# A fused attention and mixture-of-experts kernel: the last token group's gating and the first expert products take other places, and two weight splits another engine

## The chip, the cores and the metric

The kernel runs on one core of a Trainium2 chip. The metric is the device time of one execution in microseconds (us). The core's engines run side by side, each in its own instruction order, and wait for each other through semaphores: PE (TensorE: matmuls and transposes), DVE (VectorE), ACT (ScalarE), POOL (GpSimd, which also issues the indirect, row-by-row transfers) and SP, which issues most plain transfers.

## The reference

Linear attention with decay over 4 batches, 8 heads, 768 positions and a head size of 64 gives 3072 tokens of width 512. A noisy top-2 gate then picks two of 8 experts for each token, and each expert is a two-layer network 512 - 1024 - 512:

```
logits = x @ w_gate
noisy_logits = logits + log1p(exp(x @ w_noise)) * noise
top2 = argpartition(-noisy_logits, 2)[:, :2]      # two experts a token
top2_w = softmax over the two
for e in experts:
    h = maximum(x[mask] @ w1[e], 0)
    out[mask] += top2_w[mask] * (h @ w2[e])
```

## The kernel before

**Attention** runs in 12 steps (`NST`, t = 0 to 11), each of two chunks of 128 tokens. Step t's outputs `xo` are taken from PSUM by ACT (L388). Then come `products` (PE L416: the gate's two weight matrices times `xo`; ACT copies the result to `xp`), `turn_x` (8 PE transposes L428 to token rows `xc`), `store_x` (the rows go to `x_tok` in DRAM) and `logits` (PE L447: transposes into the PSUM tile `pL`).

**Routing** works on three groups of 8 chunks. `gate` is a chain of some 50 small DVE instructions (L457, the copy from `pL`, to L498, which writes `ob`). `count` (PE L532 to L537) needs `ob` and numbers the tokens of each expert. `route` (DVE L548 to L612) makes positions; in its middle `finish` issues 24 small PE products (L583), which give the row indices of expert 0's tokens. Then 16 indirect scatters per group (POOL L622) write a record of each token and choice to the list `lst`, 48 in all. `routing` is a generator: `advance(n)` emits its next n DVE instructions at that place of the program, so the FILL numbers say how gate instructions lie between other work.

**Expert 0** starts right after attention, in three passes of 2, 2 and 3 row tiles of 128 tokens. Tile rows are gathered by POOL (L813, `gather_rows`) into `xg`, turned by PE (`trans_rows`, L822) and split into a high part `xth` (ACT) and a low part `xtl` (DVE L825). All expert products are made of three: high x high, low x high, high x low. A pass has 8 columns f (`mm1`, PE L860, 12 matmuls each) into four PSUM buffers `pS`; `evac1` takes each out, the high part of `ht` by ACT (L866), the low part by DVE (L870). `gemm2` (L898, 24 matmuls a tile) follows. Weights come as fp32 in `wst`; ACT writes their high parts (L771, `split_high`) and DVE or POOL the low parts (L775, `split_low`).

**Order and pacing.** Each engine runs the program's order. Before the change the order after the last step is: `products(11)`, `trans_rows` of tiles 0 and 1, `logits(11)`, column 0 (`head[0]`), `turn_x(11)`, column 1, the second group's index products, columns 2 to 7 with the last group's gate between their evacuations on DVE, `gemm2` of tile 0, `count`, `trans_rows` of tiles 2 and 3, `gemm2` of tile 1. The second pass follows: column 0, the last group's index products L583, column 1, and so on. The scatters are spread over the columns: `paced` has POOL copy one element of a fresh `ht` column into `spacer` (L670) before it scatters. After the last scatter, SP loads the record list of the next expert (`rec`), and POOL gathers that expert's rows by it.

Of the kernel before, what the change touches and what calls it, by code (L numbers as in the profile page):

```python
# [31 lines left out]
C = 128  # L32
# [9 lines left out]
TS = 128  # L42
TAILS = (64, 64, 32, 32, 32, 0, 0, 0)
TAIL = max(TAILS)
PARTS0 = (2, 2, 3)
# [9 lines left out]
NST = NCH // 2  # L55
# [1 line left out]
MAXOV = 40  # L57
MAXT = 24
FILLA, FILLB, FILLC = {4: 24, 5: 24, 6: 20, 7: 20, 8: 19, 9: 19, NST - 1: 24}, 2, 4
FILL1, FILL2 = 4, 9  # L60
LOADS = {2: [(1, 0)], 3: [(1, 1)], 4: [(1, 2)], 5: [(1, 3)], 9: [(2, 0), (2, 1)], 10: [(2, 2)], 11: [(2, 3)]}
HIGH = {4: [(1, 0)], 5: [(1, 1)], 6: [(1, 2)], 7: [(1, 3)], 10: [(2, 0), (2, 1)]}
LOW = {5: [(1, 0)], 6: [(1, 1)], 7: [(1, 2)], 10: [(2, 0)]}
# [4 lines left out]
GB = (0, 8, 16, NCH)  # L68
NG = len(GB) - 1
# [14 lines left out]
def size(e, t):  # L84
    return TS if t < NT - 1 else TAILS[e]


def sub(ap, offset, dims):
    return bass.AP(tensor=ap.tensor, offset=ap.offset + offset, ap=dims)
# [27 lines left out]
def kernel(  # L117
# [3 lines left out]
    nc = tc.nc  # L121
# [163 lines left out]
    def finish(b, all_scattered=True):  # L285
        while "done" not in RT.get(b, {}):
            advance(1)
        if all_scattered:
            scatter(len(scatters))

    def scatter(n):
        for job in scatters[:n]:
            scatter_list(*job)
        del scatters[:n]
# [117 lines left out]
    def products(u):  # L412

        p = psum.tile([128, 2, C], FT, name="pR")
        for d in range(DB):
            nc.tensor.matmul(p[d * 32:(d + 1) * 32], wgn[:, d, :], XO[u][:, :, d, :], start=True, stop=True)  # L416
        XP[u] = aw.tile([128, 2, C], FT, name="xp", bufs=1)
        nc.scalar.activation(XP[u], p, AF.Copy)
# [3 lines left out]
    def turn_x(u):  # L422

        XC[u] = aw.tile([128, 2, DB, C], FT, name="xc")
        for a in range(2):
            p = bank()
            for d in range(DB):
                nc.tensor.transpose(p[:, d, :], XO[u][:, a, d, :], identf)  # L428
            nc.scalar.activation(XC[u][:, a], p, AF.Copy)

    def store_x(u):

        queue = nc.gpsimd if u < NST - 4 else nc.sync
        queue.dma_start(x_tok[2 * u * C:2 * (u + 1) * C, :].rearrange("(a p) m -> p a m", a=2),
                          XC[u].rearrange("p a d i -> p a (d i)"))
# [319 lines left out]
    def split_w(which, e, j, half=None, low=nc.vector):  # L755

        split_high(which, e, j, half)
        split_low(which, e, j, half, low)
# [14 lines left out]
    def split_low(which, e, j, half=None, low=nc.vector):  # L773
        st, hi, lo = split_parts(which, e, j, half)
        low.tensor_tensor(lo, st, hi.bitcast(FT), op=SUB)  # L775
# [42 lines left out]
    def trans_rows(t, n):  # L818

        p = psum.tile([128, DB, n], FT, name="pS", bufs=4)  # L820
        for d in range(DB):
            nc.tensor.transpose(p[:, d, :], XG[t][:n, d * 128:(d + 1) * 128], identf[:n, :n])  # L822
        hi, lo = [xt(i, slice(t * TS, t * TS + n)) for i in range(2)]
        nc.scalar.activation(hi, p, AF.Copy)
        nc.vector.tensor_tensor(lo, p, hi.bitcast(FT), op=SUB)  # L825
# [29 lines left out]
    def mm1(e, t0, n, f):  # L855
        cs, fs = columns(e, t0, n), slice(f * 128, (f + 1) * 128)
        p = psum.tile([128, cs.stop - cs.start], FT, name="pS", bufs=4)
        for d in range(DB):
            for i, (a, b) in enumerate(((0, 0), (0, 1), (1, 0))):
                nc.tensor.matmul(p, W1[a][d][:, fs], xt(b, cs)[:, d], start=(d == 0 and i == 0),  # L860
                                 stop=(d == DB - 1 and i == 2))
        return p
# [74 lines left out]
    for t in range(NST):  # L937
        u = t + 1
        if t:
            products(t - 1)  # L940
            turn_x(t - 1)
            if t == 8:
                split_low(1, 0, 3, low=nc.gpsimd)
        if u < NST:
            trans_k(u)
        load(t + 3, "kt")
        if u < NST:
            trans_q(u)
        load(t + 3, "qt")
        if u < NST:  # L950
            kv(u)
        if t:
            store_x(t - 1)
            paced(1, XC[t - 1][:, 1, 0, :])
        kdecay(t + 2)
        if u == NST:
            scatter(1)
        if u == NST:
            logits(t - 1)
        intra(t)  # L960
        load(t + 3, "vt")
        inter(t, 0)
        evac_o(t)
        paced(1, XO[t][:, 1, 0, :])
        if t and u < NST:
            logits(t - 1)
        if 2 * t in GB[1:]:
            if 2 * t > GB[1]:
                finish(GB.index(2 * t) - 2, False)
            jobs.append(routing(GB.index(2 * t) - 1))  # L970
        advance(FILLB)
        if u < NST:
            scores(u)
            inter(u, 1)
        for which, j in HIGH.get(t, []):
            split_high(which, 0, j)
        if u < NST:
            if LOW.get(t):
                nc.gpsimd.tensor_copy(spacer, AT[u][0][0:1, 0, 0, 0, 0:1])
            for which, j in LOW.get(t, []):  # L980
                split_low(which, 0, j, low=nc.gpsimd)
            paced(1, AT[u][1][:, 1, 0, 0, :])
        advance(FILLA.get(t, 18))
        for which, j in LOADS.get(t, []):
            load_w(which, 0, j)
        zero_out(ZEROS.get(t, 0))
        if t == 2:
            turn_noise()
        if t == 4:
            for i in range(4):  # L990
                nc.sync.dma_start(sub(lst, i * 128 * LI * RW, [[LI * RW, 128], [1, LI * RW]]), linit)
    products(NST - 1)
    for j in range(2):
        trans_rows(j, TS)
    logits(NST - 1)
    head = [mm1(0, 0, PARTS0[0], 0)]
    turn_x(NST - 1)
    store_x(NST - 1)
    head.append(mm1(0, 0, PARTS0[0], 1))
    att.close()  # L1000
    hp = ctx.enter_context(tc.tile_pool(name="hp", bufs=1, reuse_waits="tile"))
    HT.append(hp.tile([128, FB, 2 * CAP], FR, name="ht"))
    for t in range(NT):
        if t >= len(XG):
            XG.append(hp.tile([128, DM], FT, name=f"xg{t}"))
        PV.append(hp.tile([128, DM], FT, name=f"pv{t}"))
    split_low(2, 0, 1)
    for f in range(2):
        evac1(0, 0, PARTS0[0], f, head[f])
    scatter(sum(job[0] == 0 for job in scatters))  # L1010
    load_rec(0, 0)
    finish(1, False)
    for t in range(2, 4):
        gather_rows(0, t, GB[2] * C)
    scatter(1)
    jobs.append(routing(NG - 1))

    for i, (t0, n) in enumerate(parts(0)):
        for f in range(FB):
            if i or f >= 2:  # L1020
                gemm1(0, t0, n, f)
            if i == 0:
                if 1 <= f < 5:
                    split_w(2, 0, 2 + (f > 2), (f - 1) % 2)
                if f == 2:
                    nc.scalar.activation(XG[6], zero, AF.Copy)
                advance(FILL1)
            if i == 1 and f < 4:
                advance(FILL2)
                if f == 3:  # L1030
                    finish(2, False)
            if i or f >= 2:
                paced(1 + (i == 2), ht(0, 0, f, columns(0, t0, n)).bitcast(FT))
            if i == 1 and f == 2:
                load_rec(0, 1)
            if i == 2 and f == 2:
                load_rec(1, 0)
                load_rec(0, 2)
                load_rec(0, 3)
                for j in range(1, 3):  # L1040
                    load_rec(1, j)
                for t in range(NT):
                    gather_rows(1, t)
            if i == 2 and f >= 4:
                for j in X1[f - 4]:
                    trans_rows(j, size(1, j))
        if i == 0:
            zero_out(NTOK // 128)
            advance(50)
        if i == 1:  # L1050
            which_expert(1, nc.sync)
            which_list(1, nc.sync)
            for j in range(4):
                load_w(1, 1, j)
        if i == 2:
            for t in range(t0):
                scatter_out(0, t, PV[t])
        for t in range(t0, t0 + n):
            if i < 2:
                paced(3, PV[t - 1] if t > t0 else ht(0, 0, FB - 1, columns(0, t0, n)).bitcast(FT))  # L1060
            gemm2(0, t)
            if t == 0:
                advance(50)
            for j in {0: (2, 3), 2: (4, 5, 6)}.get(t, ()):
                trans_rows(j, size(0, j))
            if i == 2:
                scatter_out(0, t, PV[t][:size(0, t), :])
            if i == 2:
                for j in range((0, 2, 4)[t - t0], (2, 4, 4)[t - t0]):
                    split_w(1, 1, j)  # L1070
                    load_w(2, 1, j)
                for j in X1[t]:
                    trans_rows(j, size(1, j))
# [180 lines left out]
```

## Time and profile before

| | |
|---|---|
| time, three runs | median 722.18 us (721.09 to 722.67) |
| profiled execution: its span, which is the only time shown for it | 732.3 us |
| PE busy | 705.6 us, 96% of the span |
| DVE, ACT, POOL busy | 356.6, 237.9, 291.0 us |
| mean granted TensorE clock | 0.983 of full speed |

The profile follows one execution. A timeline row gives an instruction's start, its length, engine, line and operands, and in brackets how long the engine had been idle before it and what released it. Matmuls are pipelined, so that rows of PE overlap; the distance of two starts is what one costs. [...]

### The profile page before, as it was taken

What the parts mean: (1) busy time and instruction counts of PE and PEld (TensorE: products, weight loads), DVE (VectorE), ACT (ScalarE), POOL (GpSimd) and SP (SyncE); (2) the same over time, 40 slices, a digit from 0 to 9 for tenths busy, and PEclk for the clock granted to TensorE, in tenths of its full rate; (3) what the DMA queues carried; (4) which work ended last, traced back from release to release, by engine and by line L of the source; (5) the groups of instructions that cost most, each with busy time, mean ns of one, the idle gap of its engine ahead of it and who ended that gap; (6) DMA issues with size and microseconds to landing.
All of it is one profiled execution on the core that took longest, in us unless ns stands there. A gap on an engine that the chain in (4) does not pass through costs nothing.

```text
span 732.3 us, 13486 instructions
## 1 busy us (share of the span) xinstructions
PE 705.6 (96%) x4909; PEld 602.5 (82%) x4909; DVE 356.6 (49%) x808; ACT 237.9 (32%) x451; POOL 291.0 (40%) x454
## 2 busy tenths in 40 slices
PE   7999989798998999999999999999999999999996
PEld 5888878697896798798879887988888898889885
DVE  6446948677424556464436443634453444435211
ACT  1677756331121423042214230423132332214100
POOL 6110545567847354524163406233412433221311
PEclk8999989989999999999999999999999999999999
DMA  9999998673516556856365637565465556540211
GB/s 204 216 234 228 244 232 216 184 255 78 120 19 217 186 161 187 256 151 187 122 231 161 188 101 248 153 187 194 145 176 159 192 184 188 165 147 14 79 43 38
DMA packets 137658, 122.50 MB, mean 167 GB/s; under 512 B 87642, under 2 KB 106458, under 8 KB 137588
## 3 DMA queue, kind: packets, MB, share of 16 engines
q1 hardware_dynamic: 122660, 80.50, 41.2%
q0 software_dynamic: 14512, 40.57, 17.5%
q8 instruction: 40, 0.66, 0.4%
q10 hardware_dynamic: 416, 0.53, 0.2%
q14 instruction: 30, 0.25, 0.1%
HBM read 87.15 MB, written 35.55 MB: 168 GB/s over the span
## 4 chain that ended last, share of the span: by engine, by line
PE 74%; issue 6%; DVE 6%; DMA 6%; SPq 2%; ACT 2%; POOL 2%; another core or an unknown queue 1%; POOLq 0%; ACTq 0%; DVEq 0%
PE pS L860 34%; PE pKV L898 14%; PE pO L898 13%; PE pS L355 2%; SPq L153 2%; DMA kt<-in_k_dram 2%; PE pKV L368 2%; PE pO L903 2%; PE pO L368 1%; PE pS L428 1%; DMA out_dram<-ot,rec 1%; PE pKV L903 1%; ACT kd L340 1%; DMA vt<-in_v_dram 1%
## 5 line engine op out<-in xcount | busy, mean ns | idle before, releaser
L860 PE MATMUL pS<-xtl,w1h 128*128 128x512 f32 (+3 forms) x544 | 181.3, 333 | 1.7 <-DVE xtl L825 1.6
L860 PE MATMUL pS<-xth,w1h 128*128 128x512 f32 (+3 forms) x544 | 181.6, 334 | 1.1 <-DVE xtl L825 1.0
L860 PE MATMUL pS<-xth,w1l 128*128 128x512 f32 (+3 forms) x544 | 181.0, 333 | 0.0
L866 ACT ACTIVATE ht<-pS 128x512 fp32r<-128x512 f32 (+3 forms) x136 | 65.1, 483 | 220.4 <-PE pS L860 154.0
L870 DVE SCALAR_TENSOR_TENSOR ht<-pS,ht 128x256 fp32r<-128x256 f32 (+3 forms) x176 | 76.0, 453 | 110.7 <-ACT ht L866 99.8
L898 PE MATMUL pKV<-w2h,ht 128*128 128x512 f32 x384 | 124.2, 395 | 0.1
L898 PE MATMUL pO<-w2h,ht 128*128 128x512 f32 x384 | 122.7, 391 | 0.0
L860 PEld LDWEIGHTS pS<-xtl,w1h 128*128 128x128 f32 x544 | 103.3, 190 | 11.3 <-DVE xtl L825 2.3
L860 PEld LDWEIGHTS pS<-xth,w1h 128*128 128x128 f32 x544 | 103.2, 190 | 10.5 <-DVE xtl L825 1.2
L917 POOL DMA_INDIRECT out_dram<-ot,rec x46 | 62.8, 1364 | 121.3 <-DVE ot L910 108.5
L860 PEld LDWEIGHTS pS<-xth,w1l 128*128 128x128 f32 x544 | 103.3, 190 | 8.7
L898 PEld LDWEIGHTS pKV<-w2h,ht 128*128 128x128 f32 x384 | 72.9, 190 | 17.0 <-DVE ot L910 0.5
L898 PEld LDWEIGHTS pO<-w2h,ht 128*128 128x128 f32 x384 | 72.1, 188 | 16.1
L813 POOL DMA_INDIRECT xg<-x_tok,rec x46 | 51.6, 1123 | 62.5 <-DMA rec<-lst 46.8
L898 PE MATMUL pKV<-w2l,ht 128*128 128x512 f32 x192 | 76.2, 397 | 0.0
L898 PE MATMUL pO<-w2l,ht 128*128 128x512 f32 x192 | 75.4, 393 | 0.0
L882 POOL DMA_INDIRECT pv<-out_dram,rec x46 | 47.8, 1040 | 28.3 <-issue 28.3
L622 POOL DMA_INDIRECT lst<-recs,dest x48 | 48.7, 1014 | 11.1 <-issue 9.3
L1168 POOL COPY spacer<-ht 1x1 f32<-1x1 f32 x53 | 9.4, 177 | 103.4 <-ACT ht L866 103.3
L910 DVE SCALAR_TENSOR_TENSOR ot<-pKV,rec,pv 128x512 f32<-128x512 f32 x21 | 15.8, 751 | 63.0 <-PE pKV L898 43.3
L846 ACT ACTIVATE xth<-xg 128x512 fp32r<-128x512 f32 (+1 forms) x39 | 22.4, 599 | 72.1 <-DMA xg<-turned 71.9
L910 DVE SCALAR_TENSOR_TENSOR ot<-pO,rec,pv 128x512 f32<-128x512 f32 x21 | 15.8, 750 | 61.3 <-PE pO L898 47.0
(229 smaller groups left out, 950.4 us busy)
## 6 DMA issues: line engine op xcount, KB each, us to landing
wst<-in_moe_w_dram SPq DMA_DIRECT2D x48, 512.0 KB
turned<-ot SPq DMA_DIRECT2D x36, 256.0 KB
xg<-turned SPq DMA_DIRECT2D x144, 64.0 KB
wst<-in_moe_w_dram SPq DMA_DIRECT2D x32, 256.0 KB
kt<-in_k_dram SPq DMA_DIRECT2D x24, 256.0 KB
qt<-in_q_dram SPq DMA_DIRECT2D x24, 256.0 KB
vt<-in_v_dram SPq DMA_DIRECT2D x24, 256.0 KB
x_tok<-xc POOLq DMA_DIRECT2D x8, 512.0 KB
```

Source lines behind the costliest of these rows:

```text
L368: nc.tensor.matmul(PO[u][a][half(g), hp, :], lhs, rhs, start=n == 1, stop=n == (8 if u % NW or a else 4))
L622: st = nc.gpsimd.indirect_dma_start(out=lst, out_offset=bass.IndirectOffsetOnAxis(ap=r["dest"][:, i, c:c + 1], axis=0), in_=r["rec"][:, c, ...
L813: nc.gpsimd.indirect_dma_start(out=XG[t][:size(e, t)], out_offset=None, in_=x_tok[:rows, :], in_offset=bass.IndirectOffsetOnAxis(ap=at, ax ...
L846: nc.scalar.activation(hi, p, AF.Copy)
L860: nc.tensor.matmul(p, W1[a][d][:, fs], xt(b, cs)[:, d], start=(d == 0 and i == 0), stop=(d == DB - 1 and i == 2))
L866: nc.scalar.activation(ht(e, 0, f, cs), p, AF.Relu)
L870: nc.vector.scalar_tensor_tensor(ht(e, 1, f, c), p[:, r], 0.0, ht(e, 0, f, c).bitcast(FT), op0=OP.max, op1=SUB)
L882: nc.gpsimd.indirect_dma_start(out=PV[t][:size(e, t), :], out_offset=None, in_=out, in_offset=bass.IndirectOffsetOnAxis(ap=REC[e, t][:, 0: ...
L898: nc.tensor.matmul(p, ht(e, a, f, cs), W2[b][f // 2][:, f % 2, :], start=(i == 0), stop=(i == len(terms) - 1))
L903: nc.tensor.matmul(p[:2 * n, :], HT[0][:, f, FULL:FULL + 2 * n], W2[b][f // 2][:, f % 2, :], start=(i == 0), stop=(i == 2 * FB - 1))
L910: nc.vector.scalar_tensor_tensor(o, p, w, pv, op0=MULT, op1=ADD)
L917: st = nc.gpsimd.indirect_dma_start(out=out, out_offset=bass.IndirectOffsetOnAxis(ap=REC[e, t][:, 0:1], axis=0), in_=o, in_offset=None, bo ...
```

## The change

```diff
-FILL1, FILL2 = 4, 9
+FILL0, FILL1, FILL2 = 12, 5, 9
...
             products(t - 1)
             turn_x(t - 1)
+            if u == NST:
+                for j in range(2):
+                    trans_rows(j, TS)
...
+    finish(1, False)
+    head = [mm1(0, 0, PARTS0[0], 0)]
     products(NST - 1)
-    for j in range(2):
-        trans_rows(j, TS)
+    turn_x(NST - 1)
+    split_low(2, 0, 1, low=nc.gpsimd)
     logits(NST - 1)
-    head = [mm1(0, 0, PARTS0[0], 0)]
-    turn_x(NST - 1)
     store_x(NST - 1)
+    jobs.append(routing(NG - 1))
+    advance(FILL0)
     head.append(mm1(0, 0, PARTS0[0], 1))
...
-    split_low(2, 0, 1)
+    for t in range(2, 4):
+        gather_rows(0, t, GB[2] * C)
+    split_high(2, 0, 2)
+    split_low(2, 0, 2, low=nc.gpsimd)
+    scatter(sum(job[0] == 0 for job in scatters))
+    load_rec(0, 0)
     for f in range(2):
         evac1(0, 0, PARTS0[0], f, head[f])
-    scatter(sum(job[0] == 0 for job in scatters))
-    load_rec(0, 0)
-    finish(1, False)
-    for t in range(2, 4):
-        gather_rows(0, t, GB[2] * C)
-    scatter(1)
-    jobs.append(routing(NG - 1))
+        advance(FILL1)
...
             if i == 0:
-                if 1 <= f < 5:
-                    split_w(2, 0, 2 + (f > 2), (f - 1) % 2)
+                if 3 <= f < 5:
+                    split_w(2, 0, 3, f - 3)
...
             gemm2(0, t)
+            for j in {0: (2, 3), 2: (4, 5, 6)}.get(t, ()):
+                trans_rows(j, size(0, j))
             if t == 0:
                 advance(50)
-            for j in {0: (2, 3), 2: (4, 5, 6)}.get(t, ()):
-                trans_rows(j, size(0, j))
```

The first two tiles' rows are turned one step earlier. The second group's index products and column 0 stand ahead of `products(11)`, and `logits(11)` and the last group's gate follow at once. Of four low weight parts that DVE made here, two whole ones (`split_low(2, 0, 1)` and `(2, 0, 2)`, 128 x 1024 each) are POOL's. Gathers 2 and 3 stand ahead of four remaining scatters. Two lines more flush scatters before the record loads, which the last `paced` calls had done.

On PE, the end of attention before: the last state products (L368), the gate products (L416), the row turns of tiles 0 and 1 (`xg_330`, `xg_331`), the logits, column 0, and the turns of `xo`:

```order
L368 MATMUL pKV<-qTs,S_171 64x128
L416 MATMUL pR<-xo,wgn 32x256 x4
L822 MATMUL pS<-identf,xg_330 128x128 x4
L822 MATMUL pS<-identf,xg_331 128x128 x4
L447 MATMUL pL<-sel,xp 128x16 x2
L860 MATMUL pS<-xth_326,w1h_310 128x256
...
L860 MATMUL pS<-xth_326,w1l_317 128x256
L428 MATMUL pS<-identf,xo 128x128 x8
L860 MATMUL pS<-xth_326,w1h_310 128x256
```

And after the change, in three places: the row turns between the previous step's `xo` turns and its logits, the index products behind the last state products, and the gate products behind column 0:

```order
L822 MATMUL pS<-identf,xg_330 128x128 x4
L822 MATMUL pS<-identf,xg_331 128x128 x4
L447 MATMUL pL<-sel,xp 128x16 x2
L368 MATMUL pO<-at,vt 64x128 x2
...
L368 MATMUL pKV<-qTs,S_171 64x128
L583 LDWEIGHTS wst
L583 MATMUL pL<-tokab,wst 128x2
...
L860 MATMUL pS<-xth_326,w1l_317 128x256
L416 MATMUL pR<-xo,wgn 32x256 x4
L428 MATMUL pS<-identf,xo 128x128 x8
L447 MATMUL pL<-sel,xp 128x16 x2
L860 MATMUL pS<-xth_326,w1h_310 128x256
```

The row turns moved ahead of step 10's logits, and the index products and column 0 stand between the last state product and L416.

Also on PE, after the change, `count` of the last group (L532 to L537) in the first pass, between columns 5 and 6 (`w1l_317` ends a column, `w1h_310` starts the next):

```order
L860 MATMUL pS<-xth_326,w1l_317 128x256
L532 LDWEIGHTS lstrict
L532 MATMUL pL<-ob,lstrict 128x64
L534 LDWEIGHTS ones
L534 MATMUL pL<-ob,ones 128x56
...
L537 MATMUL pL<-ob,ones 128x8
L860 MATMUL pS<-xth_326,w1h_310 128x256
```

It stood behind the pass's first `gemm2`, L898, before; PE can't start column 6 until `ob` is written.

On POOL, the scatters (L622, with the memset L621) and gathers (L813) around the end of attention, before:

```order
L670 COPY spacer<-xo 1x1
L621 MEMSET spacer 1x1
L622 DMA lst<-recs,dest 29696x2
...
L622 DMA lst<-recs,dest 29696x2
L813 DMA xg_2406<-x_tok,idx_187 128x512
L813 DMA xg_2408<-x_tok,idx_187 128x512
```

And after:

```order
L670 COPY spacer<-xo 1x1
L621 MEMSET spacer 1x1
L622 DMA lst<-recs,dest 29696x2
L775 TENSOR_TENSOR w2l_323<-wst,w2h_319 128x1024
L813 DMA xg_2464<-x_tok,idx_187 128x512
L813 DMA xg_2466<-x_tok,idx_187 128x512
L775 TENSOR_TENSOR w2l_324<-wst,w2h_320 128x1024
L621 MEMSET spacer 1x1
L622 DMA lst<-recs,dest 29696x2
```

Two whole low parts stand on POOL, the first right behind the scatter that follows `xo`, the second behind the gathers; the other scatters come after them.

On DVE after the change, the end of the last group's gate (maximum search L486, index search L489, one-hot L495, `ob` L498) with the column evacuations L870 and the two halves of low part 3 that DVE keeps:

```order
L870 SCALAR_TENSOR_TENSOR ht<-pS,ht 128x256
L486 MAX mx<-nl 128x8 x2
L489 MAX_INDEX mi<-mx,nl 128x8 x3
L870 SCALAR_TENSOR_TENSOR ht<-pS,ht 128x256
L775 TENSOR_TENSOR w2l_325<-wst,w2h_321 128x512
L489 MAX_INDEX mi<-mx,nl 128x8 x5
L870 SCALAR_TENSOR_TENSOR ht<-pS,ht 128x256
L775 TENSOR_TENSOR w2l_325<-wst,w2h_321 128x512
L492 CAST ei<-mi 128x8x2
L495 TENSOR_TENSOR oh<-iota_172,ei 128x128
L498 TENSOR_TENSOR ob<-oh 128x64
L870 SCALAR_TENSOR_TENSOR ht<-pS,ht 128x256
```

Before, these instructions stood behind the evacuations of columns 2 to 7 and four such halves; now five evacuations and two halves lie between the gate's start and `ob`.

## Rows read from the trace of the kernel before

**Rows 1.** The page's first line: span and instructions of the profiled execution.
```profile
span 732.3 us, 13486 instructions
```

**Rows 2.** PE's waits, 128 to 260 us: in total, times, longest.
```profile
PE pS L822 <- DMA xg<-x_tok,rec: 3.0, 2, 2.2
...
PE pS L860 <- DVE xtl L825: 2.6, 2, 1.6
...
PE pL L532 <- DVE oh L495: 0.4, 1, 0.4
```

**Rows 3.** PE timeline at the end of attention: start, length, instruction, [idle before].
```profile
137.83 0.59 PE L447 MATMUL pL<-sel,xp 128*128 128x16 f32 x4 [1.18 <-DVE pos L566]
...
143.61 0.64 PE L416 MATMUL pR<-xo,wgn 128*32 128x256 f32 x8 [2.70 <-ACT xo L388]
144.18 1.97 PE L822 MATMUL pS<-identf,xg 128*128 128x128 f32 x8
```

**Rows 4.** Windows: length, busy PE PEld DVE ACT POOL, PEclk, DMA share, GB/s.
```profile
144.20:150.90 6.70, 6.54 (x32) 6.13 (x29) 2.52 (x3) 1.58 (x3) 5.47 (x9) 0.50 0.63 205
226.10:229.40 3.30, 3.30 (x10) 2.56 (x9) 0.69 (x1) 2.49 (x3) 2.56 (x3) 0.50 1.02 375
```

**Rows 5.** PE timeline, expert 0's first two passes.
```profile
153.64 0.39 PE L860 MATMUL pS<-xth,w1h 128*128 128x256 f32 x1
...
162.38 0.39 PE L898 MATMUL pO<-w2h,ht 128*128 128x512 f32 x1
...
168.41 0.19 PE L532 MATMUL pL<-ob,lstrict 128*128 128x64 bf16 x1 [0.37 <-DVE oh L495]
...
168.81 1.07 PE L822 MATMUL pS<-identf,xg 128*128 128x128 f32 x8
169.64 0.48 PE L898 MATMUL pKV<-w2h,ht 128*128 128x512 f32 x1
...
175.23 0.28 PE L860 MATMUL pS<-xth,w1h 128*128 128x256 f32 x1
...
178.51 0.55 PE L583 MATMUL pL<-tokab,wst 128*128 128x2 bf16 x16
...
179.34 0.39 PE L860 MATMUL pS<-xth,w1h 128*128 128x256 f32 x1
```

**Rows 6.** DVE timeline: first and last gate instruction of the last group.
```profile
155.36 0.28 DVE L457 COPY l<-pL 128x128 f32<-128x128 f32 x1
...
168.13 0.22 DVE L498 TENSOR_TENSOR ob<-oh 128x64 bf16<-128x64 f32 x1
```

**Rows 7.** DVE instructions by line, 155.3 to 168.4 us: count, busy, mean ns, idle.
```profile
L775 DVE TENSOR_TENSOR w2l<-wst,w2h 128x512 fp32r<-128x512 f32 x4 | 2.7, 678 | 0.0
L870 DVE SCALAR_TENSOR_TENSOR ht<-pS,ht 128x256 fp32r<-128x256 f32 x6 | 2.5, 414 | 0.0
```

**Rows 8.** POOL timeline: two weight low parts during attention.
```profile
86.65 2.36 POOL L775 TENSOR_TENSOR w1l<-wst,w1h 128x1024 fp32r<-128x1024 f32 x1
...
135.09 2.35 POOL L775 TENSOR_TENSOR w2l<-wst,w2h 128x1024 fp32r<-128x1024 f32 x1
```

**Rows 9.** DVE timeline: two instructions in those stretches, and the same two alone.
```profile
88.08 0.96 DVE L518 TENSOR_SCALAR ws<-we 128x8 f32<-128x8 f32 x1
...
136.38 1.09 DVE L564 TENSOR_SCALAR past<-past,base 128x8 f32<-128x8 f32 x1
...
141.01 0.17 DVE L518 TENSOR_SCALAR ws<-we 128x8 f32<-128x8 f32 x1
...
174.47 0.23 DVE L564 TENSOR_SCALAR past<-past,base 128x8 f32<-128x8 f32 x1
```

**Rows 10.** POOL timeline: a scatter, the first gather of 2 and 3, a paced spacer.
```profile
144.40 0.98 POOL L622 DMA_INDIRECT lst<-recs,dest  x1 [0.39 <-issue]
...
154.90 1.04 POOL L813 DMA_INDIRECT xg<-x_tok,idx  x1 [4.15 <-issue]
...
206.45 0.18 POOL L670 COPY spacer<-ht 1x1 f32<-1x1 f32 x1 [1.84 <-ACT ht L866]
```

More of the change, by code (lines that the diff above doesn't have):

```diff
@@ L1034 @@
             if i == 1 and f == 2:
+                scatter(sum(job[0] < 2 for job in scatters))
                 load_rec(0, 1)
             if i == 2 and f == 2:
+                scatter(len(scatters))
                 load_rec(1, 0)
```

## The prediction

> **What bounds the kernel now.** I read the page first: PE is the engine on the path. The profiled execution spans 732.3 us [rows 1], with PE busy for 96% of it by the table above, so a change is worth what it does to PE's waits and to PE's clock around the places it touches. The span is 10.1 us over the median of the timed runs, 722.18; I assume that this difference is the same for both kernels, make the sum in the trace's own times, and put it on the median. Then the waits of PE in the stretch that changes: it waits little, in four places [rows 2, 3]. The first is 2.70 us for `xo` behind the last state product. [...]
>
> **The reference point.** All of the moved work lies between the last state product, which ends at 143.61 - 2.70 = 140.91, and column 1 of the second pass, which starts behind the last group's index products at 179.34 [rows 3, 5]. Both kernels do the same work on PE in between, and the order behind it differs little. So I ask when the changed kernel gets to that column.
>
> **PE to the gate.** The turns of tiles 0 and 1 move into the 1.18 us in which PE waits ahead of step 10's logits [rows 3]. At full clock eight such turns take 169.64 - 168.81 = 0.83 us [rows 5], so that wait hides them; without that cover they cost 0.83. Their two `xtl` come on DVE behind the instruction that released the logits, and are needed only for column 0. Then the index products, 179.34 - 178.51 = 0.83, and column 0, (162.38 - 153.64)/6 = 1.46 [rows 5], run from 140.91 to 143.20, inside the wait for `xo`. That leaves 0.41 us of it, and L416 starts at 143.61 as before. With the gate products 0.57 (144.18 - 143.61) [rows 3], the turns of `xo` 0.83 (the same eight transposes) and the logits 0.59 [rows 3], all at full clock, the logits end at 145.6. The gate started at 155.36 before [rows 6]; it can start 9.8 us earlier.
>
> **The gate on DVE.** From its first instruction to the end of `ob` it took 168.13 + 0.22 - 155.36 = 13.0 us [rows 6], with six evacuations of 0.41 and four halves of low parts of 0.68 among it [rows 7]. Now there are five and two, so 13.0 - 0.4 - 1.4 = 11.2, and `ob` would be ready at 156.8.
>
> **The two parts on POOL.** A whole part takes 2.35 us there [rows 8]. Its place is right behind the scatter that ends at 145.38 [rows 10], so it runs from 145.4 to 147.7; the second follows two gathers of about 1.3 us, from 150.3 to 152.7. Both lie in the gate. What does that do to DVE? While POOL made such a part, a tiny DVE instruction that takes 0.23 alone took 1.09, and one of 0.17 took 0.96; each ended within 0.03 us of the end of POOL's part (137.47 against 137.44, and 89.04 against 89.01) [rows 8, 9]. They were held until POOL was done. So the rows alone show surcharges of 0.86 and 0.79, only because these two came late in the part. The bounds are 0 (the gate's instructions of other kinds slip through) and the whole of what the gate meets: its second instruction, ready at about 145.9, held until 147.7, which is 1.8, and 2.35 for the second part, 4.15 together. I take 4.15, since the held ones ended with POOL and the gate is a chain of the same kind of small SBUF instruction. `ob` is then ready at 161.0.
>
> [...]
>
> **From `ob` on.** In the changed order PE has columns 1 to 5 between the logits and `count`: 145.6 + 5 x 1.46 = 152.9. There it must wait for `ob`, 3.9 us without a hold and 8.1 with it (part of this may show at columns 4 and 5 instead, whose PSUM buffers DVE must empty between the gate's instructions). Columns 6 and 7, both `gemm2` and the rest of the pass are queued behind. After `ob`: `count` 0.40 (168.81 - 168.41), columns 6 and 7 2.92, `gemm2` 5.59 (175.23 - 169.64), turns 0.83, index products 0.83, `gemm2` 5.59, column 1.46 [rows 5]; together 17.6. The reference point is reached at 178.6 with the hold, 174.4 without, against 179.34: 0.7 or 4.9 us earlier. In this the old waits are gone: 2.3 of the 2.70, the half clock behind it (3.35), the 0.4 for `oh` and the 1.6 for `xtl` [rows 2, 3, 4], since the turns of tiles 2 and 3 now come before DVE's rest of `advance(50)`. Not in it is the clock behind the new wait. A wait of 2.7 and one of 3.0 in two pieces were each followed by 0.50; the new one is longer, so I expect 0.50 behind it too, at 1.65 to 3.35 us, 2.5 in the middle. Bounds: nothing, and 3.35.
>
> **The sum.** 2.5 - 0.7 = 1.8 us slower: 722.18 + 1.8 = **724.0 us** (734.1 in a profile). With the bounds of the clock, 0.95 to 2.65 slower.
>
> **What I cost at nothing.** ACT writes part 2 whole instead of in halves, the same elements. Gathers 2 and 3 come earlier than at 154.90, and their rows are not needed before the first `gemm2` ends. POOL gains 4.7 us of work, but it idled 4.15 us ahead of those gathers and 1.84 ahead of a spacer of the third pass [rows 10], together 6.0; behind that the last scatters are tied to PE's columns as before. If that cover is gone, see the last rival.
>
> **Rivals.** (a) *POOL holds DVE little.* What decides is the total hold: below 4.9 - 2.5 = 2.4 us the change wins. For it: the held rows are two, of one kind of operation, and much of the gate is of other kinds. Without any hold 2.5 - 4.9 = -2.4: 719.8, and 717.3 if the clock stays up too. (b) *The hold is there, but the clock comes back at once,* as the columns 1 to 5 spread the wait into pieces: 0.7 faster, 721.5. Against it: a wait in two pieces cost a stretch of half clock [rows 2, 4]. (c) *Expert 1's row wait vanishes,* if the scatters, relative to PE, come earlier by the 3.0 us: 3.0 + 1.65 less, 719.4. Against it: they are paced by columns, which shift with PE. (d) *POOL's backlog reaches the last scatter.* If only the 1.84 absorbs the 4.7, the record list and expert 1's rows come 2.9 later: 726.9.
>
> **How the numbers follow.** The forecast has a chance of 0.50, (a) 0.22, (b) 0.10, (c) 0.08, (d) 0.10. About 0.2% (1.44 us) is what a measurement of this kernel can tell from no change. Of the forecast's 0.50, 0.35 lies above 723.62 and 0.15 within; (a) is faster but for 0.03; (b) within but for 0.02; (c) faster, (d) slower. So faster 0.29, same 0.26, slower 0.45. The range from 718.8 to 726.6 leaves out the low end of (a) and the high end of (d), and little else; the forecast's own is 723.1 to 724.8.
>
> **What would show it.** In the changed profile: index products and column 0 inside the wait for `xo`, L416 still at about 143.6, and no 0.50 between 144 and 151. L457 at about 145.6 on DVE; L460 ending with POOL's first L775, and another gate instruction ending with the second. `ob` at about 161 and a PE wait for it of up to 8 us in the first pass, with 0.50 behind. Column 1 of the second pass within 2 us of 179.3 plus the clock's cost. Wrong if no gate instruction is stretched (then a), if the clock is 1.00 behind `count` (b), or if PE's wait for expert 1's rows is no longer 3.0 us (c, d).

## The result, and the profile after

| | before | changed |
|---|---|---|
| median of nine runs | 722.67 us (721.09 to 728.42) | 729.57 us (726.6 to 732.45) |
| ratio | | 1.007, 95% interval 1.0043 to 1.0098 |
| profiled execution: span | 732.3 us | 727.8 us |
| its own time | not shown | 729.57 us |

The change makes the kernel slower by 0.7%, by this ratio some 5.1 us (3.1 to 7.1); the plain medians differ by 6.9. The forecast was 1.8 us slower, range 718.8 to 726.6: the sign is right, the size is not, and the time lies outside the range. And the two spans say the opposite of the times. The changed kernel's own time is 1.8 us above its span; if it is so for before, its profiled execution took about 734 us, longer than any of the nine timed ones. That trace was of an unusual execution.

The page of the changed kernel, span and busy times:

```profile
span 727.8 us, 13486 instructions
...
PE 703.1 (97%) x4909; PEld 600.7 (83%) x4909; DVE 359.1 (49%) x805; ACT 237.4 (33%) x450; POOL 292.7 (40%) x456
```

PE's waits after the change, 130 to 260 us, answering to [rows 2] (in total, times, longest):

```profile
PE pL L532 <- DVE ob L498: 4.0, 1, 4.0
PE pS L822 <- DMA xg<-x_tok,rec: 2.9, 2, 2.1
PE pS L860 <- DVE ht L870: 2.5, 1, 2.5
PE pL L583 <- issue: 0.8, 2, 0.5
```

The waits for `xo`, for `oh` and for `xtl` are gone as forecast, and the wait for expert 1's rows (L822) is 2.9 us as before. In their place stand 4.0 us ahead of `count` and 2.5 us at column 4, whose PSUM buffer DVE had not emptied. The places on PE, answering to [rows 3, 5]: gate products, logits, column 4, `count`, and column 1 of the second pass, which was the prediction's reference point:

```profile
138.68 0.64 PE L416 MATMUL pR<-xo,wgn 128*32 128x256 f32 x8
...
140.18 0.52 PE L447 MATMUL pL<-sel,xp 128*128 128x16 f32 x4
...
147.57 0.39 PE L860 MATMUL pS<-xth,w1h 128*128 128x256 f32 x1 [2.47 <-DVE ht L870]
...
156.15 0.21 PE L532 MATMUL pL<-ob,lstrict 128*128 128x64 bf16 x1 [3.97 <-DVE ob L498]
...
176.44 0.28 PE L860 MATMUL pS<-xth,w1h 128*128 128x256 f32 x1
```

On DVE, answering to [rows 6, 9]: the first two gate instructions, a group of four in its middle, and the last:

```profile
140.73 0.29 DVE L457 COPY l<-pL 128x128 f32<-128x128 f32 x1 [1.90 <-PE pL L447]
141.06 1.13 DVE L460 TENSOR_SCALAR zc<-l 128x64 f32<-128x64 f32 x1
...
143.44 3.74 DVE L110 SCALAR_TENSOR_TENSOR gacc<-gacc,gu 128x64 f32<-128x64 f32 x4
...
155.87 0.22 DVE L498 TENSOR_TENSOR ob<-oh 128x64 bf16<-128x64 f32 x1
```

And POOL's two low parts (compare [rows 8]):

```profile
139.73 2.40 POOL L775 TENSOR_TENSOR w2l<-wst,w2h 128x1024 fp32r<-128x1024 f32 x1
...
144.73 2.36 POOL L775 TENSOR_TENSOR w2l<-wst,w2h 128x1024 fp32r<-128x1024 f32 x1
```

The same two in the trace of before:

```profile
155.68 0.26 DVE L460 TENSOR_SCALAR zc<-l 128x64 f32<-128x64 f32 x1
...
158.66 0.99 DVE L110 SCALAR_TENSOR_TENSOR gacc<-gacc,gu 128x64 f32<-128x64 f32 x4
```

The hold is there. L460 takes 1.13 us where it took 0.26, and ends at 142.19, with POOL's first part (142.13). The four L110 take 3.74 us where four took 0.99, and end at 147.18, with the second part (147.09). That is 3.6 us in all; 4.15 was forecast.

Two windows of the changed kernel (columns as in [rows 4]), behind the wait at column 4 and behind `count`:

```profile
148.90:151.60 2.70, 2.70 (x15) 2.63 (x14) 2.39 (x12) 0.90 (x2) 2.26 (x5) 0.50 0.03 1
156.70:161.80 5.10, 5.10 (x27) 5.10 (x25) 2.95 (x4) 0.38 (x1) 2.77 (x7) 0.50 1.06 359
```

Half clock follows each of the two waits, 2.7 and 5.1 us long. Behind `count` the starts of column 6's matmuls lie 0.213 us apart, against 0.12 for column 3 at 1.00. With half of each stretch counted as extra, an estimate, this is about 3.9 us of extra PE time (3.4 by those two distances), where one stretch with 2.5 us extra was forecast.

### The profile page after: what moved, and what is told of

Same layout as the page of the kernel before. It is cut to its first block, busy times and chain, and to the rows that moved or that the text cites. A ratio compares the mean times of both kernels' runs of the same rounds, so it can differ in the third digit from the quotient of the medians.

```text
span 727.8 us, 13486 instructions
## 1 busy us (share of the span) xinstructions
PE 703.1 (97%) x4909; PEld 600.7 (83%) x4909; DVE 359.1 (49%) x805; ACT 237.4 (33%) x450; POOL 292.7 (40%) x456
## 4 chain that ended last, share of the span: by engine, by line
PE 79%; issue 5%; DMA 4%; DVE 4%; SPq 3%; POOL 2%; POOLq 1%; ACT 1%; ACTq 0%; DVEq 0%
PE pS L860 35%; PE pKV L898 14%; PE pO L898 14%; PE pS L355 2%; PE pKV L368 2%; SPq L153 2%; PE pO L368 2%; PE pO L903 2%; PE pS L428 1%; POOLq L1180 1%; PE pKV L903 1%; PE pS L312 1%; PE pS L325 1%; DMA out_dram<-ot,rec 1%; POOL out_dram L917 1%
## 5 line engine op out<-in xcount | busy, mean ns | idle before, releaser
L870 DVE SCALAR_TENSOR_TENSOR ht<-pS,ht 128x256 fp32r<-128x256 f32 (+3 forms) x176 | 76.1, 453 | 112.1 <-ACT ht L866 107.7
L898 PE MATMUL pKV<-w2h,ht 128*128 128x512 f32 x384 | 123.2, 392 | 1.6 <-DVE ot L910 1.6
L898 PE MATMUL pO<-w2h,ht 128*128 128x512 f32 x384 | 123.0, 391 | 0.0
L898 PEld LDWEIGHTS pKV<-w2h,ht 128*128 128x128 f32 x384 | 72.1, 188 | 18.3 <-DVE ot L910 2.0
L898 PEld LDWEIGHTS pO<-w2h,ht 128*128 128x128 f32 x384 | 72.3, 188 | 16.2
L898 PE MATMUL pO<-w2l,ht 128*128 128x512 f32 x192 | 75.6, 393 | 0.0
L898 PE MATMUL pKV<-w2l,ht 128*128 128x512 f32 x192 | 75.5, 393 | 0.0
L813 POOL DMA_INDIRECT xg<-x_tok,rec x46 | 51.5, 1119 | 59.4 <-DMA rec<-lst 21.5
L622 POOL DMA_INDIRECT lst<-recs,dest x48 | 47.8, 995 | 12.4 <-issue 10.3
```

Of the source, the lines that this page charges most:

```text
L622: st = nc.gpsimd.indirect_dma_start(out=lst, out_offset=bass.IndirectOffsetOnAxis(ap=r["dest"][:, i, c:c + 1], axis=0), in_=r["rec"][:, c, ...
L813: nc.gpsimd.indirect_dma_start(out=XG[t][:size(e, t)], out_offset=None, in_=x_tok[:rows, :], in_offset=bass.IndirectOffsetOnAxis(ap=at, ax ...
L870: nc.vector.scalar_tensor_tensor(ht(e, 1, f, c), p[:, r], 0.0, ht(e, 0, f, c).bitcast(FT), op0=OP.max, op1=SUB)
L898: nc.tensor.matmul(p, ht(e, a, f, cs), W2[b][f // 2][:, f % 2, :], start=(i == 0), stop=(i == len(terms) - 1))
```

## The experiments

One number is taken from every trace: the distance from the start of the last state product (L368) to column 1 of the second pass. In the first trace of before it is 179.34 - 140.64 = 38.7 us, in the changed kernel 176.44 - 134.94 = 41.5. The kernels of one group ran on one chip, and their ratios are to before on that chip. A trace is one execution, whose own time can be off the median by up to 3.3 us (the traced one of the second before took 725.37 us, the slowest of its ten; that of the first late count 717.71, against a median of 720.82).

| run | last L368 | second pass | distance | median, ratio (95% interval) |
|---|---|---|---|---|
| group 1: before | 134.44 | 172.13 | 37.7 | 722.79, 0.9987 (0.997 to 1.0005) |
| change, parts on DVE | 134.60 | 174.10 | 39.5 | 724.81, 1.0018 (0.9989 to 1.0047) |
| before, parts on POOL | 135.96 | 175.58 | 39.6 | 725.72, 1.0031 (1.0007 to 1.0055) |
| before, wait filled | 135.53 | 174.31 | 38.8 | 723.57, 1.001 (0.998 to 1.004) |
| group 2: late count, DVE | 134.58 | 166.31 | 31.7 | 720.82, 0.9964 (0.9921 to 1.0008) |
| late count, POOL | 138.78 | 173.25 | 34.5 | 725.91, 1.0025 (1.0003 to 1.0047) |
| change, kept warm | 134.84 | 174.94 | 40.1 | 732.1, 1.0124 (1.0099 to 1.015) |
| change | 134.55 | 175.82 | 41.3 | 728.4, 1.0083 (1.005 to 1.0116) |
| group 3: before, lean | 134.79 | 168.32 | 33.5 | 716.75, 0.9997 (0.9979 to 1.0014) |
| late count, DVE, lean | 136.02 | 167.01 | 31.0 | 715.79, 0.9987 (0.9968 to 1.0005) |
| late count, POOL, lean | 134.75 | 169.79 | 35.0 | 718.57, 1.0023 (1.0002 to 1.0044) |
| change, lean | 134.47 | 175.99 | 41.5 | 725.88, 1.0129 (1.0099 to 1.016) |
| group 4: before | 134.90 | 167.92 | 33.0 | 716.17, 0.9989 (0.997 to 1.0008) |
| change | 135.59 | 176.67 | 41.1 | 724.36, 1.0093 (1.0068 to 1.0118) |
| late count, DVE | 139.16 | 169.87 | 30.7 | 717.6, 1.0 (0.9978 to 1.0022) |

**The kernel before, again** (no edit).

> The kernel before, unchanged, timed against itself and profiled again. The profile shown of before spans 732.3 us, 4.5 us more than that of the change, although the timed runs of before are 0.7% faster. Theory A (the first profile was an untypical execution, late by some 5.7 us in attention steps 6 to 10): the new profile spans about 721 us, and its last xo of attention lies near 137 us instead of 142.5. Theory B (a profile of before is always longer than its timed runs): about 732 us again. The ratio is 1.000, and its interval says what a 0.2% difference is worth.

Theory A holds: the span was 723.6 us, and the last state product came at 134.44 instead of 140.64, near the changed kernel's 134.94. So 6.2 us of the first trace's span were lost ahead of the stretch that the distance measures.

**The change with the parts on DVE.**

```diff
-    split_low(2, 0, 1, low=nc.gpsimd)
...
-    split_low(2, 0, 2, low=nc.gpsimd)
+    split_low(2, 0, 1)
     for f in range(2):
         evac1(0, 0, PARTS0[0], f, head[f])
...
+                if 1 <= f < 3:
+                    split_low(2, 0, 2, f - 1)
```

> The change with its two low weight parts back on DVE: part 1 (1.22 us) ahead of the first two evacuations, part 2 in two halves (0.6 each) behind columns 1 and 2. If POOL's hold of DVE costs what the prediction says (about 4 us of gate, of which DVE's own making of the parts gives back 2.4), this is 1 to 2 us faster than the change, with a PE wait for the gate about 1.7 us shorter. Rival (the hold is not the point, the long PE wait and the half clock behind it are): the same as the change within 1 us. Rival (the loss lies outside this stretch): the same as the change, 727 to 729 us.

The distance falls by 2.0 us to 39.5, as the first theory says, and the ratio by some 0.5% (from the first result to this group's) to a time not clear of before's. Behind the last state product `ob` is ready at 19.6 us instead of 21.2. PE's waits are not the 1.7 us shorter that were expected: the one at column 4 is gone, but PE then waits 6.2 us at `count`, against 6.5 in two places. With no part on POOL the group of four runs undisturbed, DVE's L110 in this kernel:

```profile
142.16 1.01 DVE L110 SCALAR_TENSOR_TENSOR gacc<-gacc,gu 128x64 f32<-128x64 f32 x4
```

**Before with the parts on POOL.**

```diff
-    split_low(2, 0, 1)
+    split_low(2, 0, 1, low=nc.gpsimd)
...
-                if 1 <= f < 5:
-                    split_w(2, 0, 2 + (f > 2), (f - 1) % 2)
+                if 1 <= f < 3:
+                    split_high(2, 0, 2, f - 1)
+                if f == 2:
+                    split_low(2, 0, 2, low=nc.gpsimd)
+                if 3 <= f < 5:
+                    split_w(2, 0, 3, f - 3)
```

> The kernel before with only its two low weight parts moved to POOL: part 1 behind the scatter that follows xo, part 2 behind the second half of its high part, in the gate of the last group. If POOL holds DVE, the gate gets up to 2.35 us longer less the 1.2 us of halves that DVE no longer makes, and PE waits 1 to 1.5 us longer ahead of count: 1 to 2 us slower than before. Rival (DVE is not held for the whole part): the same or up to 1 us faster, as DVE has 2.4 us less to do.

DVE's group of four in this kernel, and under it POOL's part:

```profile
153.97 3.94 DVE L110 SCALAR_TENSOR_TENSOR gacc<-gacc,gu 128x64 f32<-128x64 f32 x4
```

```profile
155.15 2.41 POOL L775 TENSOR_TENSOR w2l<-wst,w2h 128x1024 fp32r<-128x1024 f32 x1
```

2.95 us more than 0.99; POOL's part ends at 157.56, the group 0.35 us behind it. The distance grows by 1.9 us and the median by 2.9: moving the two parts alone makes the kernel slower, though it takes work off DVE. The 1.9 us of this trace are not the hold's alone. Its half clock behind the wait for `xo` lasts 10.2 us, where the first 6.5 us behind that wait ran at 0.56 in group 1's before:

```profile
138.20:148.40 10.20, 9.37 (x45) 8.16 (x46) 1.38 (x2) 3.47 (x8) 7.80 (x12) 0.50 0.52 170
```

The gate starts 15.9 us behind the last state product instead of 14.6, and only then is it 1.6 us longer (14.6 against 12.9).

**Before with only the wait filled.**

```diff
+            if u == NST:
+                for j in range(2):
+                    trans_rows(j, TS)
...
+    finish(1, False)
+    head = [mm1(0, 0, PARTS0[0], 0)]
     products(NST - 1)
-    for j in range(2):
-        trans_rows(j, TS)
-    logits(NST - 1)
-    head = [mm1(0, 0, PARTS0[0], 0)]
     turn_x(NST - 1)
+    logits(NST - 1)
...
-    finish(1, False)
```

> The kernel before with only the early row turns, and the second group's index products and column 0 ahead of the last gate products; the last group's gate and the low parts stay where they were. If the wait for xo and the half clock behind it cost what the profile shows (2.3 and 3.35 us) and nothing takes their place, PE reaches the first pass's end some 5 us earlier, but the gate then starts with the evacuations and PE waits for it at count: 2 to 4 us faster than before. Rival (the gate's end sets the pace whatever PE does ahead of it): within 1 us of before.

The time is the rival's: same as before. Its trace shows the wait for `xo` gone and other PE waits in its place, and a later stretch at half clock:

```profile
PE pS L860 <- issue: 2.6, 4, 1.0
PE pS L860 <- DVE xtl L825: 2.0, 1, 2.0
```

```profile
150.60:156.40 5.80, 5.80 (x27) 5.80 (x28) 5.02 (x16) 3.66 (x9) 4.34 (x9) 0.50 1.05 384
```

`ob` was ready at 161.95 - 135.53 = 26.4 us behind the last state product, against 27.6 in before: the gate ended only 1.2 us sooner. But the rival's reason is not shown: PE does not wait for `ob` at all here, and the time gained goes to the new waits and the new stretch at half clock.

**Late count, parts on DVE.** The change with the parts on DVE as above, and

```diff
-FILL0, FILL1, FILL2 = 12, 5, 9
+FILL0, FILL1, FILL2 = 12, 3, 9
```

> The change with the two low parts back on DVE, and the gate spread thinner (3 gate steps a column instead of 5), so that count comes behind the first tile's gemm2 and row turns as before, while the gate still starts early. If PE's wait for the gate inside the columns and the half clock behind it are the loss, none is left, and the fill of the xo wait is pure gain: 4 to 6 us faster than before, 717 to 719 us. Rival (filling the wait gains nothing here, as the run with only the fill came out like before): 722 to 724 us.

PE waits neither for `xo` nor for `ob`, and the distance is 31.7 us, the shortest of the first two groups. In time it was 0.36% faster than before, some 2.6 us where 4 to 6 were expected, with an interval that just takes in 1; the repeat in group 4 decides below.

**Late count, parts on POOL.** The same numbers in the change itself.

> The same late count with the two low parts on POOL as in the change. DVE is still held for about 3.6 us by the parts, but the gate has slack now. If the hold costs only through the gate's end, this is within 1 us of the run with the parts on DVE, 717 to 719 us. Rival (the hold also delays the evacuations, and columns 4 and 5 wait for their PSUM buffers): 2 to 3 us slower than that run, 720 to 722 us, with a PE wait for ht in the waits.

The rival: 2.8 us more distance and 5.1 us more time than with the parts on DVE (the leaner pair of group 3: 4.0 and 2.8). PE's waits for the evacuation and for expert 1's rows in this kernel:

```profile
PE pS L860 <- DVE ht L870: 2.6, 1, 2.6
PE pS L822 <- DMA xg<-x_tok,rec: 2.6, 2, 2.0
```

So the parts on POOL cost time even where the gate has slack. Of this the trace shows the wait of 2.6 us for a PSUM buffer that DVE empties; with the parts on DVE, in group 4's trace, it is 0.8.

**The change kept warm.** Nothing of the result is changed.

```diff
+    def stay_warm(n):
+        p = psum.tile([128, PARTS0[0] * TS], FT, name="pR")
+        for _ in range(n):
+            nc.tensor.matmul(p, W1[0][0][:, :128], xt(0, slice(0, PARTS0[0] * TS))[:, 0], start=True, stop=True)
...
     def count(b):
+        if b == NG - 1:
+            stay_warm(26)
...
+            if i == 0 and f == 4:
+                stay_warm(16)
```

> The change with dummy matmuls (a weight tile times the first tiles' rows into a PSUM tile that nobody reads) in front of column 4 (16, 1.9 us) and in front of count (26, 3.1 us), inside PE's two waits; the outputs are untouched. If the half clock behind count costs what the profile shows (columns 6 and 7 at 0.213 us a matmul instead of 0.119 for 5.3 us), this is 2 to 3 us faster than the change. Rival (the waits set the pace and the clock comes back anyway, or the dummies delay count): the same as the change or up to 2 us slower.

Windows of this kernel, from the logits to the dummies ahead of `count`, and behind `count`:

```profile
140.50:150.60 10.10, 9.53 (x77) 9.13 (x77) 9.40 (x26) 4.67 (x10) 9.00 (x10) 1.00 0.69 175
156.50:159.30 2.80, 2.80 (x17) 2.80 (x15) 1.41 (x2) 0.00 (x0) 2.36 (x7) 0.50 1.05 287
```

The clock stays at 1.00 through the first wait, and the half clock behind `count` lasts 2.8 us instead of 5.1. The distance falls by 1.2 us only, yet the four timed runs are 3.7 us slower than the change beside it. Its trace has a wait of 2.7 us for `xtl` of expert 1 which the change's has not. What the half clock costs in time stays open.

**The change, again** (no edit).

> The change itself once more, on the same chip as the other three. If the 0.7% is a property of the kernel and not of the chip it ran on, 726 to 730 us, ratio 1.004 to 1.010; the trace of the change shows 3.7 us more than a typical one of before, so about 1.005 if that trace is typical.

Ratio 1.0083: the loss belongs to the kernel.

**Leaner scatters.** In the four kernels before, late count on DVE, late count on POOL, and the change:

```diff
-    def scatter_list(b, c, i):
+    def scatter_list(b, c, i, spaced=False):
...
-        nc.gpsimd.memset(spacer, 0.0)
+        if not spaced:
+            nc.gpsimd.memset(spacer, 0.0)
...
-            scatter(n)
+            scatter(n, True)
```

> The kernel before without the memset of a scatter that stands right behind a paced spacer copy (about 0.25 us of POOL each, some 30 of them): POOL's chain up to the last scatter gets shorter, nothing else changes. Theory P (POOL's chain of scatters sets when expert 1's rows come, and that is what the faster versions lose behind the second pass): here POOL waits for a column ahead of the third pass's scatters, so little is gained, 0 to 1 us: 722 to 723 us. Rival N (the loss behind the second pass is something else): no change either.

> The run with the late count and the parts on DVE, with the leaner scatters. In its trace PE was 6 us earlier than before at the second pass, and POOL never waited for a column ahead of the last scatters: POOL was the limit. Theory P: the relief of 4 to 5 us of POOL comes through, up to 3 us faster than that run, 717 to 719 us, 0.7% faster than before. Rival N: the same as that run, 720.8 us.

> The run with the late count and the parts on POOL, with the leaner scatters. Theory P: POOL's 4.7 us of added work are balanced by the 4 to 5 us of relief, so it falls from 725.9 to 721 to 723 us. Rival N: 725 to 726 us again.

> The change itself with the leaner scatters. Its loss up to the second pass (3.7 us against a typical before) stays. Theory P: the other 2 us, which the traces don't show at the second pass, go: 726 to 727 us instead of 728.4 to 729.6. Rival N: 728 to 730 us.

Theory P gets no support: late count on DVE gains no more against before than in group 2, late count on POOL stands at 1.0023 as without the relief (1.0025), and the change at 1.0129. But before itself differs here: its distance is 33.5 us, not 37.7 as in group 1, and its median 716.75, so groups 2 and 3 are not one comparison. Group 4, where before is like this one, has the late count without the relief at 1.0 (0.9987 here) and the change at 1.0093: no gain from the relief there either. And in the change a DVE instruction is stretched even ahead of the gate, in the second group's index work (a 64 x 1 addition that took 0.15 in before, 2.94 here):

```profile
137.21 2.94 DVE L593 TENSOR_TENSOR found<-found,found 64x1 f32<-64x1 f32 x1
```

The logits, which share `pL` with that work, wait 2.4 us for it.

**Three kernels on one chip.** No edits to before and the change; late count on DVE as above.

> The kernel before once more, for its trace on the same chip as the next two. Theory S (the size of the loss is set by before's own wait for xo): the trace shows either a wait of some 2.6 us with half clock behind it, and the second pass at 37 to 39 us behind the end of attention, or one of some 1.2 us at full clock, and 33 to 34 us. Ratio 1.000.

> The change once more. Its second pass is at 41 to 42 us behind the end of attention whatever the chip, since DVE's gate sets it. Theory S: the timed difference to before is the difference of the two traces there, within 1.5 us: 3 to 4 us if before shows the long wait, 7 to 9 us if it shows the short one. Rival (what is lost lies behind the second pass): the timed difference is more than 1.5 us off that.

> The late count with the parts on DVE once more, the one version that was faster than before. Second pass at 31 to 32 us. Theory S: 5 to 6 us faster than before where before shows the long wait, 2 to 3 us where it shows the short one. Rival (POOL's chain or the rows of expert 1 take it back): less than 1 us faster.

In before, the gate products on PE and the window behind them, answering to [rows 3, 4]:

```profile
136.42 0.64 PE L416 MATMUL pR<-xo,wgn 128*32 128x256 f32 x8 [1.25 <-ACT xo L388]
```

```profile
137.00:143.50 6.50, 5.67 (x52) 5.32 (x49) 2.81 (x4) 2.83 (x6) 5.41 (x9) 1.00 0.79 275
```

The same two in the kernel before of group 1:

```profile
137.30 0.64 PE L416 MATMUL pR<-xo,wgn 128*32 128x256 f32 x8 [2.59 <-ACT xo L388]
```

```profile
137.90:144.40 6.50, 6.33 (x35) 5.93 (x32) 2.42 (x3) 1.83 (x4) 5.44 (x9) 0.56 0.56 193
```

A wait of 1.25 us at full clock against one of 2.59 with 0.56 behind it, from one and the same kernel on two chips. In the change, PE's waits:

```profile
PE pL L532 <- DVE ob L498: 6.0, 2, 5.2
PE pS L860 <- DVE ht L870: 2.3, 1, 2.3
PE pL L447 <- ACT w2h L771: 1.7, 1, 1.7
```

DVE's two held instructions, and POOL's parts:

```profile
138.80 2.52 DVE L606 SCALAR_TENSOR_TENSOR dest<-ei,pp 128x16 int32<-128x16 f32 x1
...
143.31 3.02 DVE L101 TENSOR_SCALAR gn<-gn 128x64 f32<-128x64 f32 x1
```

```profile
138.91 2.36 POOL L775 TENSOR_TENSOR w2l<-wst,w2h 128x1024 fp32r<-128x1024 f32 x1
...
143.85 2.41 POOL L775 TENSOR_TENSOR w2l<-wst,w2h 128x1024 fp32r<-128x1024 f32 x1
```

In the first changed trace both are undisturbed:

```profile
138.32 0.17 DVE L606 SCALAR_TENSOR_TENSOR dest<-ei,pp 128x16 int32<-128x16 f32 x1
...
142.71 0.19 DVE L101 TENSOR_SCALAR gn<-gn 128x64 f32<-128x64 f32 x1
```

In group 4 they end with POOL's parts (141.27 and 146.26), 5.2 us longer in all. The logits' wait of 1.7 us belongs to it: the row names ACT, but L447 starts at 141.60, right behind the index work on DVE (L606, L608, L610) that the first part held. Theory S holds for the change: the distances differ by 41.1 - 33.0 = 8.1 us, the medians by 724.36 - 716.17 = 8.2, and by the ratio the loss is 6.7 us (4.9 to 8.5). It doesn't hold for the late count: 2.3 us less distance, but no less time (ratio 1.0). In its trace 4.3 us are lost ahead of the last state product (139.16 against 134.90), as in the first trace of before; its own time was 1.9 us above the median. Its waits for expert 1's rows are a smaller part:

```profile
PE pS L822 <- DMA xg<-x_tok,rec: 1.7, 3, 0.9
PE pS L860 <- DVE ht L870: 0.8, 1, 0.8
```

So no version here is shown to beat before.

## Why the prediction was right and wrong

**Right: the changed kernel's own timeline.** Counted from the end of the last state product (0.27 us behind its start), the prediction puts the gate's start at 4.7 us, `ob` at 20.1, the second pass at 178.6 + 2.5 - 140.91 = 40.2. The trace has 5.5, 20.9 and 41.2. The gate's length with the hold was forecast at 15.4 and is 156.09 - 140.73 = 15.4; that this agrees so well is luck, since the hold is 0.5 us shorter than forecast and the rest of the gate 0.5 longer. The waits are 6.5 us together where 8.1 was the sum, part of it at column 4, as the prediction allowed. Expert 1's rows cost the same as before, so rivals (c) and (d) did not decide; nor did (a) and (b), since POOL held DVE (3.6 us in all) and the clock fell (0.50 over 5.1 us behind `count`).

**What the loss hangs on.** With the parts on POOL or on DVE, and `count` in its early or its late place, there are four versions. Their ratios to before are 1.0083 (the change in group 2), 1.0018 (parts on DVE, group 1), 1.0025 (late count, group 2) and 0.9964 (both, group 2; 1.0 in group 4). Either step alone takes most of the loss away: the hold, and PE's wait for `ob` in the middle of the pass, make it together. Both are in the prediction.

**Wrong: two terms of the sum.** The loss is 5.1 us by the ratio, where 1.8 was forecast. The traces give 3.8 of it: 41.5 us to the second pass in the changed kernel against 37.7 in the second trace of before. About 1 us of what was missed lies in the changed kernel, in the step "That leaves 0.41 us of it, and L416 starts at 143.61 as before". The index products and column 0 did not fit into the wait: PE had issue waits of 0.8 us in them, and L416 started at 138.68 - 134.94 = 3.7 us behind the last state product's start instead of 3.0. The gate was late by that 0.8. (Of the two stretches at half clock the first lies ahead of `ob` and cost nothing more; the second, 5.1 us, stands for the 2.5 of the sum.) No run shows that 2.5 as extra time, nor the 1.65 and 3.35 that it lies between: that half of a stretch at 0.50 is extra was the author's estimate. What the runs showed in its place are stretches of 2.7 and 5.1 us at 0.50, with matmuls 0.213 us apart instead of 0.12.

Another 1.0 us lies in the reference point of before, "column 1 of the second pass, which starts behind the last group's index products at 179.34": one execution, 38.7 us behind the last state product, where group 1 has 37.7. The second pass there waits 0.7 us for `xtl` instead of 1.6. With it goes "I assume that this difference is the same for both kernels": the difference of 10.1 us between span and median was itself the sign that the trace was no usual one (6.2 of it lay ahead of the stretch), and the changed kernel's is 1.8 the other way. The last 1.3 us of the 5.1 are within the interval of the measurement, and where they belong stays open; the execution in the second trace of before was itself 2.6 us above its median, and no trace shows where.

**Wrong as a constant: the credit.** The step "In this the old waits are gone: 2.3 of the 2.70, the half clock behind it (3.35), the 0.4 for `oh` and the 1.6 for `xtl`" took 7 to 8 us of savings from one trace. In group 1 most of them are there again: 2.59 us of wait for `xo`, a clock of 0.56 over the 6.5 us behind it, 0.7 us for `xtl`. In groups 3 and 4 most are not: before reaches the second pass at 33.5 and 33.0 us, in group 4's trace with 1.25 us of wait for `xo`, a clock of 1.00 over the 6.5 us behind it, and no wait for `xtl` at the second pass (the 0.4 us that group 4 has for it is at column 0 of the first). The changed kernel stands at 41 to 41.5 in all four of its traces, with POOL's hold and PE's wait for the gate in each. So by distance its loss is 3.8 us against one form of before and 8.0 to 8.1 against the other.

**What is open.** The two forms go with ACT's first `xo` copy behind the last state product. In groups 1 and 4 it stands so:

```profile
136.16 0.60 ACT L388 ACTIVATE xo<-pO 128x512 f32<-128x512 f32 x1 [5.04 <-PE pKV L368]
```

```profile
135.28 0.60 ACT L388 ACTIVATE xo<-pO 128x512 f32<-128x512 f32 x1 [3.70 <-PE pKV L368]
```

136.16 - 134.44 = 1.72 us behind that product's start in the one, 135.28 - 134.90 = 0.38 in the other. It is not a matter of one execution or of one kernel: in all ten traces of the first result and of groups 1 and 2 the copy starts 1.72 to 1.85 us behind, in all seven of groups 3 and 4 0.38, in before and in the change alike. So the form goes with the group, and with its chip as far as can be told. The first result's two traces are of the late form. Why ACT starts late was not settled, and that this alone makes the two forms is not shown, since no run moves it by itself. Nor was it settled where the late count loses its 2.3 us: filling the wait and POOL's chain of scatters were tried, and neither explains it. Three of the 17 traces, of before once and of the late count twice, lose about 4 to 6 us ahead of the last state product (it starts at 140.64, 138.78 and 139.16, in the others at 134.4 to 136.0); how often untraced executions do is not known.

## What to carry to other kernels

Before a wait is counted as savings, look at a second execution of the same kernel, and at one on another chip: a span far above the timed median (here 732.3 against 722.67 us) says that the trace is not a usual one, and a second trace on one chip changed the reference point by 1.0 us, and traces on two others by 5.2 and 5.7. A chain of small VectorE instructions on the critical path and a long elementwise instruction on GpSimd did not go side by side here (four of the chain took 3.74 us instead of 0.99 beside one of 2.36), though the move took work off VectorE. And filling a wait ahead of such a chain moved the wait to the end of the chain (6.2 us with the parts on DVE), until the product that needs the chain's end was put later as well.

## What the hardware showed that was not expected

Beside a low part on POOL small DVE instructions of several kinds took longer; the first four named here ended 0.05 to 0.09 us behind the part. In the first changed trace the TENSOR_SCALAR L460 took 1.13 instead of 0.26 us, beside a part of 2.40, and the four SCALAR_TENSOR_TENSOR L110 3.74 instead of 0.99, beside one of 2.36. In group 4's changed trace the SCALAR_TENSOR_TENSOR L606 took 2.52 instead of 0.17, beside 2.36, and the TENSOR_SCALAR L101 3.02 instead of 0.19, beside 2.41. L101 begins, as recorded, 0.54 us ahead of POOL's part. The TENSOR_TENSOR L593 took 2.94 instead of 0.15 in group 3's changed kernel, whose POOL row for that place is not shown. Not every DVE instruction beside a part was longer: the copy L457 from the PSUM tile `pL` took 0.29 us beside the first part in the changed trace, and 0.28 in before.

The same program's median was 716.2 us on one chip (group 4's before) and 722.8 on another (group 1's). And a PE wait of 1.25 us was followed by 6.5 us at 1.00 (group 4's before), one of 2.59 by 6.5 us at 0.56 (group 1's), one of 2.70 by 6.70 us at 0.50 (the first trace of before) and one of 2.47 by 1.4 us at 0.99 and then 2.7 us at 0.50 (the changed kernel, column 4). In group 4's changed kernel the wait of 2.3 us at column 4 was followed by a window of 3.9 us at 1.00:

```profile
148.90:152.80 3.90, 3.16 (x24) 3.06 (x25) 3.45 (x18) 1.29 (x3) 2.80 (x6) 1.00 0.02 1
```
